# Nine product slots of block 1 placed in the opening stage, and a changed order of splits and loads in blocks 2 to 4

## The chip, the cores and the metric

The kernel runs on one core of a Trainium2 chip. The core has a matrix engine (TensorE, PE), a vector engine (VectorE, DVE), a scalar engine (ScalarE, ACT), GpSimd (POOL) and SyncE (SP), which in this kernel only issues transfers (DMAs). Each engine works through its own list of instructions in order and waits on semaphores for the others. The metric is the device time of one execution in microseconds; less is better.

## The reference

Chunked attention with a few memory keys, then two feed-forward networks. All arrays are float32.

```python
# attention: q, k, v are (4, 8, 768, 64); 8 memory keys and values per batch and head
for c in range(24):                       # chunks of 32 queries
    k_full = concat(mem_k, k[16 left .. 8 right of the chunk])       # 64 keys
    a = softmax(q_c @ k_full.T / 8)
    out[chunk] = a @ v_full
x = out as (3072, 512)
x = max(x @ w1, x @ w2, x @ w3) @ w_mid   # w1..w3 (512, 768), w_mid (768, 512)
h = x @ w_in                              # w_in (512, 2048)
g = h if h >= 1, 0 if h <= -1, else (h + 1)**2 / 4
out = g @ w_out                           # w_out (2048, 512)
```

## The kernel before

The 3072 tokens are six blocks of 512 (block 0 to 5). The attention runs in 24 units of 128 tokens, four units to a block. A unit u has steps, named by letter: s (scores, on TensorE), mx (the row maximum and its subtraction, on VectorE), ex (exp, ScalarE), n (sum and normalization), a with ca (transpose and copy, tile aT), o with co (product with the values, copy to xs), x with cx and dx (transposes tx, and the two parts xh and xl of the result, which the network reads). tk, ck, ek, kw and tq, c0q, c1q prepare keys and queries for units 0 to 11 by transposes on TensorE. From unit 12 (TRIO0) on, keys (three units at once, gk, tile kq) and queries (two units at once, gq) are loaded in pieces that VectorE transposes itself (flip_k, flip_q, steps fk and fq). Their loads are put into a list, `queue`, from which a few are issued in each slot; flip_k and flip_q issue what is left of the whole list before they begin.

Each product of the networks is made three times from numbers that are split in a high and a low part (mm3). A slot is 12 matmuls of 512 columns. For a block j of the first network a slot l1(j, f, m) makes the product with one of three weights (m = 0, 1, 2) for one of K1 = 6 groups of columns f; ScalarE copies the first to a tile t, VectorE takes the maximum of it and the second, and then the third, and the split makes hh (a cast on ScalarE) and hl (a subtraction on GpSimd) of t. A slot l2(j, f) adds the product of that with the weight b to four accumulators, y. The results of l1 lie in ps_mm, a pool of two PSUM buffers, in turn; a buffer is free again when the copy or the maximum has read it.

The weights come as float32 and are converted before use: convert_w (an abs, on ScalarE for some, then three operations on VectorE, tile c), then hi and lo parts by hi_w, rest_w and lo_w (VectorE, ScalarE and GpSimd). Block 0's and the later blocks' 24 weights (a0, a1, a2 and b, for f = 0 to 5) are converted in an opening stage whose order is the table PLAN. There l is an l1 slot of block 0 (l16 is f = 5, m = 1), lt its copy or maximum, lh its split, m an l2 slot, wa to wp the parts of a conversion, f a weight's load. TensorE's order is that of PLAN; the order on the other engines is set by a scheduler from the order of PLAN and its own estimate of times. Behind PLAN all engines keep the order in which the code is written.

Behind PLAN, a loop goes over the slots of blocks 1 to 5. In each slot of blocks 1 to 4 it makes one attention step (att_step) and one step of the second network's 32 weights, c and d (round_step): load, convert, round, and store to wd in DRAM. In block 5 and in the second network these are loaded again and split (w_step). SyncE issues everything in the order of the code.

```python
        for s, (f, *a) in enumerate(order):
            ...
            f(*a)
            if last_block:
                ...
            else:
                att_step()
                round_step()
```

Of the kernel before, what the change touches and what calls it, by code (L numbers as in the profile page):

```python
# [37 lines left out]

PLAN = """
# [25 lines left out]
SUM_ON_ACT = [2, 5, 6, 8]  # L65


@with_exitstack
def attention_then_two_mlps(ctx, tc, q, k, v, mem_k, mem_v, w1, w2, w3, w_mid, w_in, w_out, out):
# [229 lines left out]
    def load_ks(g):  # L299
        b, s0 = divmod(3 * g, UPB)  # L300
        t0 = s0 * P - LEFT
        c0 = 1 if t0 < 0 else 0
        for h in range(HP):
            for r, a in quadrants(k[b], h, t0 + c0 * CH, CH, NB3):
                queue.append(partial(nc.sync.dma_start, out=ks[r:r + CH, h, c0:c0 + NB3, :], in_=a))
        r0, c, t = (LEFT, 0, 0) if c0 else (0, NB3, S - LEFT)
        for e in range(2):
            for x in range(2):
# [3 lines left out]
                    in_=k[b].rearrange("(h e) t d -> e t h d", e=2)[e, t:t + LEFT, :, 32 * x:32 * x + 32]))  # L312

    def load_qs(g):
        b, s0 = divmod(2 * g, UPB)
        if 2 * g == TRIO0:
            t = stage.tile([P, TB, 2], U32, tag="st", name=f"qs{g}", bufs=3)
            t = t.rearrange("p f t -> p (f t)").bitcast(F32)
        else:
            t = kT2.rearrange("p i h t -> p (i h t)")[:, 0:2 * TB]  # L320
        qs[g] = t.rearrange("p (h c d) -> p h c d", h=HP, d=CH)
        for h in range(HP):
            for r, a in quadrants(q[b], h, s0 * P, CH, 2 * NC):
                queue.append(partial(nc.sync.dma_start, out=qs[g][r:r + CH, h], in_=a))
# [9 lines left out]
    def flip_q(u):  # L334
# [122 lines left out]
    def steps(u):  # L457
# [13 lines left out]
        if u == TRIO0 - 3 or u >= TRIO0 - 1 and u % 2:  # L471
            v += [("gq", (u + 3) // 2)]
# [30 lines left out]
    hs, cur, acc = {}, {}, {}  # L503

# [7 lines left out]
    def l1_pe(j, f, m):  # L512
        cur["ps", m] = ps = ps_mm.tile([P, TB], F32, tag="mm", name=f"l1_{j}_{f}_{m}")
# [99 lines left out]
    stash, slot = [], [1]  # L613

    def round_step():
        at_step = slot[0] % 6
        slot[0] += 1
        room = 4
        if at_step in (0, 2) and stash:
# [184 lines left out]
```

## Time and profile before

| | us |
|---|---|
| median of three runs (lowest, highest) | 1088.77 (1085.14, 1095.03) |
| the profiled execution | 1090.18 |
| span in its trace | 1088.1 |
| TensorE busy | 1034.8 (95%) |
| VectorE busy | 561.9 (52%) |
| ScalarE busy | 344.3 (32%) |
| GpSimd busy | 292.9 (27%) |

The mean granted clock of TensorE is 0.985 of full speed. On the chain of work that ended last, TensorE holds 82% and VectorE 11%. Busy shares are means over stages that differ much, so a stage has to be looked at by itself.

### The profile page before, as it was taken

How to read it: one execution, taken by the hardware profiler on the slowest of the kernel's cores; microseconds unless marked ns; L12 is line 12 of the kernel's file. 1: busy time of each engine (PE TensorE's matmuls, PEld its weight loads, DVE VectorE, ACT ScalarE, POOL GpSimd, SP SyncE). 2: the span in 40 equal slices, each digit the busy share in tenths (PEclk: the TensorE clock that was granted, in tenths of full speed). 3: DMA queues.
4: the chain of work that ended last, by engine and by line, in shares of the span. 5: the costliest groups of instructions: out<-in, count | busy, mean ns of one | idle time of the engine just before them, and what ended most of it. 6: DMA issues, size and time to landing. Idle time of an engine off the chain costs nothing.

```text
span 1088.1 us, 15214 instructions
## 1 busy us (share of the span) xinstructions
PE 1034.8 (95%) x5890; PEld 841.9 (77%) x5890; DVE 561.9 (52%) x883; ACT 344.3 (32%) x640; POOL 292.9 (27%) x233
## 2 busy tenths in 40 slices
PE   4887889999999999999999999999999999999998
PEld 3665668788778887888888888888888888888886
DVE  8899984678578777666454232223223223223222
ACT  5734434333223322224343222222222222222222
POOL 5465571010001110001223322322322332332221
PEclk8998999999999999999999999999999999999999
DMA  9745335446546456335441001001001001001001
GB/s 209 182 114 142 111 89 147 103 106 186 111 125 173 125 136 156 98 113 174 127 136 30 20 16 43 20 1 49 29 1 49 20 10 49 20 1 39 1 1 39
DMA packets 164504, 89.74 MB, mean 82 GB/s; under 512 B 126800, under 2 KB 144208, under 8 KB 164432
## 3 DMA queue, kind: packets, MB, share of 16 engines
q1 hardware_dynamic: 164432, 88.77, 30.2%
q8 instruction: 46, 0.75, 0.3%
q14 instruction: 26, 0.21, 0.1%
HBM read 67.76 MB, written 20.97 MB: 82 GB/s over the span
## 4 chain that ended last, share of the span: by engine, by line
PE 82%; DVE 11%; issue 2%; DMA 2%; SPq 2%; ACT 1%; POOL 0%; DVEq 0%; ACTq 0%; POOLq 0%
PE l L499 15%; PE l L500 15%; PE l L501 15%; PE o L590 8%; PE o L589 8%; PE o L588 8%; PE y L499 3%; PE y L500 2%; PE y L501 2%; PE s L358 2%; PE o L421 1%; DVE c_a L132 1%; DVE c_a L135 1%; SPq L328 1%; DMA st_d<-in_moe_w_out_dram 1%
## 5 line engine op out<-in xcount | busy, mean ns | idle before, releaser
L576 DVE SCALAR_TENSOR_TENSOR u<-u 128x512 f32<-128x512 f32 x96 | 66.5, 692 | 357.4 <-ACT u L575 357.4
L509 POOL TENSOR_TENSOR hl_b<-u,hh_b 128x512 fp32r<-128x512 f32 x96 | 123.8, 1290 | 373.6 <-ACT hh_b L508 209.8
L499 PE MATMUL l<-xh,hi_a 128*128 128x512 f32 x432 | 176.8, 409 | 7.8 <-DVE t L525 7.8
L501 PE MATMUL l<-xh,lo_a 128*128 128x512 f32 x432 | 170.4, 394 | 0.3 <-POOL lo_a L162 0.3
L500 PE MATMUL l<-xl,hi_a 128*128 128x512 f32 x432 | 170.3, 394 | 0.0
L499 PE MATMUL l<-yh,hi_c 128*128 128x512 f32 x384 | 150.5, 392 | 0.0
L500 PE MATMUL l<-yl,hi_c 128*128 128x512 f32 x384 | 150.4, 392 | 0.0
L501 PE MATMUL l<-yh,lo_c 128*128 128x512 f32 x384 | 150.3, 391 | 0.0
L590 PE MATMUL o<-hi_d,hl_b 128*128 128x512 f32 x384 | 150.0, 391 | 0.0
L588 PE MATMUL o<-hi_d,hh_b 128*128 128x512 f32 x384 | 149.9, 390 | 0.0
L589 PE MATMUL o<-lo_d,hh_b 128*128 128x512 f32 x384 | 149.9, 390 | 0.0
L509 POOL TENSOR_TENSOR hl_a<-t,hh_a 128x512 fp32r<-128x512 f32 x36 | 48.6, 1351 | 337.0 <-ACT hh_a L508 337.0
L575 ACT ACTIVATE u<-l 128x512 f32<-128x512 f32 x96 | 57.4, 598 | 240.3 <-PE l L501 197.7
L508 ACT CAST hh_b<-u 128x512 fp32r<-128x512 f32 x96 | 59.6, 621 | 143.7 <-DVE u L577 143.7
L499 PEld LDWEIGHTS l<-xh,hi_a 128*128 128x128 f32 x432 | 82.7, 191 | 26.3 <-DVE t L525 8.9
L501 PEld LDWEIGHTS l<-xh,lo_a 128*128 128x128 f32 x432 | 82.2, 190 | 18.6 <-POOL lo_a L162 0.7
L500 PEld LDWEIGHTS l<-xl,hi_a 128*128 128x128 f32 x432 | 82.7, 192 | 15.5
L501 PEld LDWEIGHTS l<-yh,lo_c 128*128 128x128 f32 x384 | 72.2, 188 | 15.9
L500 PEld LDWEIGHTS l<-yl,hi_c 128*128 128x128 f32 x384 | 72.2, 188 | 15.8
L588 PEld LDWEIGHTS o<-hi_d,hh_b 128*128 128x128 f32 x384 | 72.1, 188 | 15.7
L499 PEld LDWEIGHTS l<-yh,hi_c 128*128 128x128 f32 x384 | 72.1, 188 | 15.6
L590 PEld LDWEIGHTS o<-hi_d,hl_b 128*128 128x128 f32 x384 | 72.1, 188 | 15.5
(137 smaller groups left out, 1420.4 us busy)
## 6 DMA issues: line engine op xcount, KB each, us to landing
st_a<-in_moe_w_dram SPq DMA_DIRECT2D x18, 512.0 KB
vw<-in_v_dram SPq DMA_DIRECT2D x160, 56.0 KB
st_c<-in_moe_w_in_dram SPq DMA_DIRECT2D x16, 512.0 KB
st_d<-in_moe_w_out_dram SPq DMA_DIRECT2D x16, 512.0 KB
yd<-y SPq DMA_DIRECT2D x24, 256.0 KB
yr<-yd SPq DMA_DIRECT2D x24, 256.0 KB
out_dram<-ob SPq DMA_DIRECT2D x24, 256.0 KB
wd<-c_c SPq DMA_DIRECT2D x16, 256.0 KB
```

The source lines that it names most:

```text
L132: V.tensor_scalar(out=cf, in0=cf, scalar1=LEAST, scalar2=MOST, op0=ALU.max, op1=ALU.min)
L358: nc.tensor.matmul(sv[r:r + 64, c // 2, 2 * (h % 2) + h // 2, :], qTb[u % 2][:, h, c].rearrange("p e t -> p (e t)"), kw[:, h, c, 0:NK], st ...
L499: nc.tensor.matmul(ps, whi, xhi, start=first, stop=False)
L500: nc.tensor.matmul(ps, whi, xlo, start=False, stop=False)
L501: nc.tensor.matmul(ps, wlo, xhi, start=False, stop=last)
L508: nc.scalar.copy(out=hi, in_=h)
L509: nc.gpsimd.tensor_tensor(out=lo, in0=h, in1=hi.bitcast(F32), op=ALU.subtract)
L575: nc.scalar.activation(out=a, in_=ps, func=AF.Relu, bias=0.5, scale=0.5)
L576: nc.vector.scalar_tensor_tensor(out=a, in0=a, scalar=1.0, in1=a, op0=ALU.min, op1=ALU.mult)
L588: nc.tensor.matmul(acc[t], hi[:, c], whi, start=first, stop=False)
L589: nc.tensor.matmul(acc[t], hi[:, c], wlo, start=False, stop=False)
L590: nc.tensor.matmul(acc[t], lo[:, c], whi, start=False, stop=last)
```

## The change

The table PLAN gets nine slots of block 1, k0 to k8 (f = 0 to 2, m = 0 to 2), with their copies and maxima (kt) and one split (kh2). Unit 5 to 7 of the attention move forward in it, since block 1 needs them. Behind PLAN, block 1 has 15 slots left (nine of l1, m5 and five of l2), in an order written out by hand, and the attention's steps are spread over them, up to two in a slot. In blocks 2 to 4 the split of a tile t is issued a slot later, behind the attention's steps, and l2 stands behind the third l1 slot instead of ahead of it. Keys are put ahead of what waits in `queue`, queries have two buffers (kT2, and two tiles y) and are asked for in even units. The weights' steps follow two short tables, BY_SLOT and BY_PART; 28 of 32 weights are stored, and the last four are converted in the second network, by w_step.

```diff
-tk6 f7 cx3 wp5 wa7 dx2 a4 f8 wh7 wp6 dx3 wg7 l0 ca4 l1 wa8 lt0 ck6 wp7 f9 o4 lv5 wa9 lt1 s5 mx5 l2
+tk6 f7 cx3 wp5 wa7 dx2 a4 f8 wh7 wp6 dx3 wg7 l0 ca4 ck6 wp7 f9 lk8 ek6 wa8 lq7 l1 lt0 f10 wg8 wh8
...
+m2 wa15 cx7 dx7 wp14 k0 wg15 wh15 f17 l11 kt0 wp15 wa16 f18 l12 lt11 wg16 lh11 wh16 wa17 lt12 k1
...
+EARLY = 3
...
         c0 = 1 if t0 < 0 else 0
+        later = queue[:]
+        del queue[:]
         for h in range(HP):
...
+        queue.extend(later)
 
     def load_qs(g):
         b, s0 = divmod(2 * g, UPB)
-        if 2 * g == TRIO0:
-            t = stage.tile([P, TB, 2], U32, tag="st", name=f"qs{g}", bufs=3)
-            t = t.rearrange("p f t -> p (f t)").bitcast(F32)
+        if g % 2:
+            t = kT2.rearrange("p i h t -> p (i h t)")
+            t = [t[:, 0:TB], t[:, TB:2 * TB]]
         else:
-            t = kT2.rearrange("p i h t -> p (i h t)")[:, 0:2 * TB]
+            t = [mx.tile([P, TB], F32, tag="y", name=f"qs{g}_{i}", bufs=2) for i in range(2)]
...
-        if u == TRIO0 - 3 or u >= TRIO0 - 1 and u % 2:
-            v += [("gq", (u + 3) // 2)]
+        if u == TRIO0 - 3 or u >= TRIO0 - 2 and u % 2 == 0:
+            v += [("gq", u // 2 + 2)]
...
         if m == 0:
-            cur["t"] = mx.tile([P, TB], F32, tag="t", name=f"t_{j}_{f}", bufs=2)
-            nc.scalar.copy(out=cur["t"], in_=ps)
+            tag = "y" if j == 1 and f < EARLY else "t"
+            cur["t", j, f] = mx.tile([P, TB], F32, tag=tag, name=f"t_{j}_{f}", bufs=2)
+            nc.scalar.copy(out=cur["t", j, f], in_=ps)
...
     def slot_l1(j, f, m):
         l1_pe(j, f, m)
         l1_max(j, f, m)
-        l1_split(j, f, m)
+        if m == 2:
+            unsplit.append((j, f, m))
...
+    def feed(room):
+        while queue and room > 0:
+            queue.pop(0)()
+            room -= 1
...
+    def round_step(acts, most):
+        if "out" in acts and stash:
             n, t = stash.pop(0)
             nc.sync.dma_start(out=wd[n - len(round1)], in_=t)
-            room -= 1
-        if at_step in (0, 2) and fetched[0] < len(conv):
+        name = conv[converted[0]][0] if raw_tiles() else None
+        if "a" in acts and name and name not in half:
+            convert_w(*name)
+        if "b" in acts and name in half:
+            stash.append((converted[0], round_w(*name)))
+            converted[0] += 1
+        if "in" in acts and fetched[0] < stashed and raw_tiles() < most:
             fetch_w(*conv[fetched[0]][0])
             fetched[0] += 1
...
+    BY_PART = "out in b", "", "out in", "a", "b", "a"
+
+    BY_SLOT = "out a", "b in", ""
...
-        order = []
-        for j in range(1, NB):
+        order = [(slot_l1, 1, 3, 0), (slot_l2, 0, 5), (slot_l1, 1, 3, 1), (slot_l2, 1, 0),
+                 (slot_l1, 1, 3, 2), (slot_l2, 1, 1), (slot_l1, 1, 4, 0), (slot_l2, 1, 2),
+                 (slot_l1, 1, 4, 1), (slot_l1, 1, 4, 2), (slot_l2, 1, 3), (slot_l1, 1, 5, 0),
+                 (slot_l1, 1, 5, 1), (slot_l2, 1, 4), (slot_l1, 1, 5, 2)]
+        first2 = len(order)
+        for j in range(2, NB):
             for f in range(K1):
-                order += [(slot_l1, j, f, 0), (slot_l1, j, f, 1),
-                          (slot_l2, *((j, f - 1) if f else (j - 1, K1 - 1))), (slot_l1, j, f, 2)]
+                l2 = [(slot_l2, *((j, f - 1) if f else (j - 1, K1 - 1)))]
+                order += [(slot_l1, j, f, 0), (slot_l1, j, f, 1)]
+                order += [(slot_l1, j, f, 2)] + l2 if j < NB - 1 else l2 + [(slot_l1, j, f, 2)]
...
+            made = unsplit[:]
             f(*a)
+            if s in (1, 3):
+                l1_split(1, 1 + s // 2, 2)
+            if last_block:
+                made = unsplit[:]
+            else:
+
+                for _ in range(-(-(len(todo) - 6 * UB * (NB - 3) + 2) // (first2 - s)) if s < first2 else 1):
+                    att_step()
+
+            for x in made:
+                l1_split(*x)
+                unsplit.remove(x)
...
-                att_step()
-                round_step()
+                if s < first2:
+                    feed(4)
+                    round_step(BY_SLOT[s % 3], 1)
+                else:
+                    part = (slot[0] + 1) % 6
+                    slot[0] += 1
+                    feed((4, 5, 3, 5, 4, 0)[part])
+                    round_step(BY_PART[part], 3)
```

What the order becomes is shown at three places. First VectorE, at the end of the opening stage, before. The tiles c_b_4, c_a2_5 and c_b_5 are the last three weights; t_0_4 is block 0's tile for f = 4, and l1_0_4_2 the product that its last maximum reads.

```order
L525 TENSOR_TENSOR t_0_4_1427<-l1_0_4_2_1464,t_0_4_1427 128x512
L135 SCALAR_TENSOR_TENSOR c_b_4_1422<-st_b_4_1416,c_b_4_1422 128x512
L148 TENSOR_SCALAR st_b_4_1416<-c_b_4_1422 128x512
L154 SCALAR_TENSOR_TENSOR st_b_4_1416<-st_b_4_1416 128x512
L132 TENSOR_SCALAR c_a2_5_1477<-c_a2_5_1477 128x512
L133 TENSOR_SCALAR c_a2_5_1477<-c_a2_5_1477 128x512
L135 SCALAR_TENSOR_TENSOR c_a2_5_1477<-st_a2_5_1429,c_a2_5_1477 128x512
L148 TENSOR_SCALAR st_a2_5_1429<-c_a2_5_1477 128x512
L131 TENSOR_SCALAR c_b_5_1571<-st_b_5_1453 128x512
```

VectorE at the same place of the changed kernel:

```order
L137 SCALAR_TENSOR_TENSOR c_a2_5_1700<-st_a2_5_1606,c_a2_5_1700 128x512
L150 TENSOR_SCALAR st_a2_5_1606<-c_a2_5_1700 128x512
L133 TENSOR_SCALAR c_b_5_1725<-st_b_5_1663 128x512
L134 TENSOR_SCALAR c_b_5_1725<-c_b_5_1725 128x512
L135 TENSOR_SCALAR c_b_5_1725<-c_b_5_1725 128x512
L137 SCALAR_TENSOR_TENSOR c_b_5_1725<-st_b_5_1663,c_b_5_1725 128x512
L150 TENSOR_SCALAR st_b_5_1663<-c_b_5_1725 128x512
L533 TENSOR_TENSOR t_0_4_1457<-l1_0_4_2_1564,t_0_4_1457 128x512
L533 TENSOR_TENSOR t_1_1_1577<-l1_1_1_1_1589,t_1_1_1577 128x512
```

The last maximum of t_0_4 moved from ahead of these weights to behind the last of them, and maxima of block 1 follow it.

Second TensorE at unit 9's transposes ta9 in block 1, before; the other nine matmuls of l1_1_2_1 and then o9 follow.

```order
L500 MATMUL l1_1_2_0_1914<-xl1_864,hi_a0_2_723 128x512
L501 MATMUL l1_1_2_0_1914<-xh1_863,lo_a0_2_724 128x512
L409 MATMUL ta9_1929<-ident_81,p9_1847 128x128 x4
L499 MATMUL l1_1_2_1_1945<-xh1_863,hi_a1_2_866 128x512
L500 MATMUL l1_1_2_1_1945<-xl1_864,hi_a1_2_866 128x512
L501 MATMUL l1_1_2_1_1945<-xh1_863,lo_a1_2_867 128x512
```

TensorE at the same place of the changed kernel:

```order
L506 MATMUL l1_1_3_2_1984<-xl1_886,hi_a2_3_1349 128x512
L507 MATMUL l1_1_3_2_1984<-xh1_885,lo_a2_3_1350 128x512
L415 MATMUL ta9_1998<-ident_81,p9_1929 128x128 x4
L427 MATMUL o9_2005<-vw_90,aT9_2003 32x2x64 x16
L505 MATMUL y1_0_1932<-hh_a1_1_1847,hi_b_1_847 128x512
L506 MATMUL y1_0_1932<-hl_a1_1_1848,hi_b_1_847 128x512
L507 MATMUL y1_0_1932<-hh_a1_1_1847,lo_b_1_848 128x512
```

The product o9 reads the copy aT9 of ta9, and moved from a slot behind ta9 to right behind it.

Third SyncE in block 1, where keys and queries of units 12 and on are loaded, before: kq are keys, kT2 and qs queries, vw the values, st_d and st_c weights to be converted, wd the store of a rounded weight.

```order
L628 DMA kq_87<-in_k_dram 32x12x32 x10
L244 DMA vw_90<-in_v_dram 56x4x64 x6
L244 DMA vw_90<-in_v_dram 48x4x64 x2
L621 DMA wd_84<-c_d_0_2140 128x512
L112 DMA st_d_1_2262<-in_moe2_w_out_dram 128x1024
L628 DMA kq_87<-in_k_dram 32x12x32 x6
L328 DMA kq_87<-in_k_dram 16x4x32 x4
L621 DMA wd_84<-c_c_3_2219 128x512
L114 DMA st_c_4_2318<-in_moe2_w_in_dram 128x4x256
```

SyncE at the same place of the changed kernel:

```order
L246 DMA vw_90<-in_v_dram 56x4x64 x6
L246 DMA vw_90<-in_v_dram 48x4x64 x2
L630 DMA kq_87<-in_k_dram 32x12x32 x4
L333 DMA kq_87<-in_k_dram 32x12x32 x4
L333 DMA kq_87<-in_k_dram 16x4x32 x4
L333 DMA kT2_85<-in_q_dram 32x8x32 x16
L642 DMA wd_84<-c_c_1_2131 128x512
L114 DMA st_d_0_2321<-in_moe2_w_out_dram 128x1024
```

The load of a weight that stood between two parts of the keys now stands behind the rest of the keys and sixteen loads of queries. On VectorE the conversion of that weight, c_d_0, stands ahead of block 1's last maximum:

```order
L452 TENSOR_TENSOR xl2_1899<-tx11_2376,xh2_1898 128x4x128
L134 TENSOR_SCALAR c_d_0_2392<-c_d_0_2392 128x512
L135 TENSOR_SCALAR c_d_0_2392<-c_d_0_2392 128x512
L137 SCALAR_TENSOR_TENSOR c_d_0_2392<-st_d_0_2321,c_d_0_2392 128x512
L369 MEMSET s12_2409 64x4x16
L376 TENSOR_REDUCE m12_2427<-s12_2409 128x8
L381 TENSOR_TENSOR p12_2429<-s12_2409,m12_2427 128x512
L171 TENSOR_SCALAR st_d_0_2321<-c_d_0_2392 128x512
L172 SCALAR_TENSOR_TENSOR st_d_0_2321<-st_d_0_2321 128x512
L173 TENSOR_TENSOR c_d_0_2392<-c_d_0_2392,st_d_0_2321 128x512
L533 TENSOR_TENSOR t_1_5_2336<-l1_1_5_2_2437,t_1_5_2336 128x512
```

The buffer of l1_1_5_2, which this maximum reads, is the one that l1_2_0_1 takes next.

## Rows read from the trace of the kernel before

**Rows 1.** Busy us by stretch: PE, PEld, DVE, ACT, POOL, then granted clock, DMA.

```profile
50.00:100.00 50.00, 40.69 (x288) 32.30 (x287) 47.80 (x69) 20.30 (x54) 28.38 (x22) 0.97 0.48 130
100.00:150.00 50.00, 37.25 (x233) 28.92 (x234) 48.74 (x67) 18.78 (x41) 33.79 (x23) 0.91 0.45 125
...
600.00:700.00 100.00, 100.00 (x440) 82.26 (x439) 26.79 (x39) 26.12 (x44) 29.43 (x23) 1.00 0.08 26
```

**Rows 2.** Waits of TensorE: total us, times, longest.

```profile
PE tx L434 <- ACT xs L428: 10.2, 4, 3.6
```

**Rows 3.** Timeline of VectorE, end of the opening stage: start, us, what.

```profile
156.20 0.41 DVE L148 TENSOR_SCALAR st_b<-c_b 128x512 uint32<-128x512 uint32 x1
156.54 0.68 DVE L525 TENSOR_TENSOR t<-l,t 128x512 f32<-128x512 f32 x1
157.65 0.69 DVE L446 TENSOR_TENSOR xl<-tx,xh 128x512 fp32r<-128x512 f32 x1 [0.44 <-ACT xh L442]
158.26 0.68 DVE L370 TENSOR_REDUCE m<-s 128x8 f32<-128x512 f32 x1
158.97 0.17 DVE L373 TENSOR_SCALAR m<-m 128x8 f32<-128x8 f32 x1
```

**Rows 4.** Timeline of TensorE from block 1's first slot to block 2's.

```profile
160.87 0.39 PE L499 MATMUL l<-xh,hi_a 128*128 128x512 f32 x1
...
163.59 0.60 PE L252 MATMUL tk<-ident,kq 128*128 128x128 f32 x4
163.95 0.48 PE L499 MATMUL l<-xh,hi_a 128*128 128x512 f32 x1
...
169.98 0.60 PE L409 MATMUL ta<-ident,p 128*128 128x128 f32 x4
...
173.26 1.08 PE L421 MATMUL o<-vw,aT 128*32 128x128 f32 x32
...
242.87 0.50 PE L499 MATMUL l<-xh,hi_a 128*128 128x512 f32 x1
```

**Rows 5.** Timelines of SP, DVE, ACT and PE, block 2, 284 to 302 us.

```profile
284.50 12.04 SPq L328 DMA_DIRECT2D kq<-in_k_dram  x20
...
295.63 0.71 DVE L331 STREAM_TRANSPOSE kw<-kq 128x512 f32<-128x512 f32 x1 [6.58 <-DMA kq<-in_k_dram]
...
300.52 0.62 ACT L508 CAST hh_a<-t 128x512 fp32r<-128x512 f32 x1 [7.87 <-DVE t L525]
...
301.67 1.12 PE L434 MATMUL tx<-ident,xs 128*128 128x128 f32 x4 [3.56 <-ACT xs L428]
```

**Rows 6.** TensorE's second wait (timeline), and stretches after the first (columns as above).

```profile
424.73 1.11 PE L434 MATMUL tx<-ident,xs 128*128 128x128 f32 x4 [2.59 <-ACT xs L428]
...
302.00:304.00 2.00, 2.00 (x8) 1.71 (x7) 1.78 (x2) 1.28 (x3) 0.68 (x1) 0.50 0.17 36
304.00:306.00 2.00, 2.00 (x9) 1.63 (x8) 1.59 (x4) 0.00 (x0) 0.00 (x0) 0.84 0.84 256
```

**Rows 7.** One operation of the conversion: ns min/median/max, first and last start.

```profile
L132 DVE TENSOR_SCALAR c_a<-c_a x18: 409/848/1507, 11.0 to 146.9; 128x512 f32<-128x512 f32 x18
```

**Rows 8.** Timeline of VectorE: unit 8's copy aT.

```profile
170.62 0.69 DVE L413 COPY aT<-ta 128x512 f32<-128x512 f32 x1 [2.56 <-PE ta L409]
```

**Rows 9.** Timelines of SP and ACT: issues, and a weight's landing.

```profile
195.64 3.55 SPq L244 DMA_DIRECT2D vw<-in_v_dram  x8
...
270.98 4.78 SPq L628 DMA_DIRECT2D kT<-in_q_dram  x10
...
167.90 0.53 SPq L114 DMA_DIRECT2D st_c<-in_moe_w_in_dram  x1
...
172.86 0.67 ACT L129 ACTIVATE c_c<-st_c 128x512 f32<-128x512 f32 x1 [2.09 <-DMA st_c<-in_moe_w_in_dram]
```

**Rows 10.** Conversion of the weights d: ns min/median/max, first and last start.

```profile
L135 DVE SCALAR_TENSOR_TENSOR c_d<-st_d,c_d x16: 691/693/694, 214.3 to 499.2; 128x512 uint32<-128x512 uint32 x16
...
L169 DVE TENSOR_SCALAR st_d<-c_d x16: 417/418/421, 215.6 to 501.0; 128x512 uint32<-128x512 uint32 x16
L170 DVE SCALAR_TENSOR_TENSOR st_d<-st_d x16: 693/695/697, 216.0 to 501.5; 128x512 f32<-128x512 uint32 x16
L171 DVE TENSOR_TENSOR c_d<-c_d,st_d x16: 692/1648/1674, 216.7 to 502.2; 128x512 f32<-128x512 f32 x16
```

More of the change, by code (lines that the diff above doesn't have):

```diff
@@ L337, in flip_q @@
         c = u % 2 * NC
-        for e in range(2):
-            r = slice(e * 64, e * 64 + 64)
-            nc.vector.transpose(out=qTb[u % 2][r, :, :, e, :], in_=qs[u // 2][r, :, c:c + NC, :])
+        for i, t in enumerate(qs[u // 2]):
+            for e in range(2):
+                r = slice(e * 64, e * 64 + 64)
+                nc.vector.transpose(out=qTb[u % 2][r, 2 * i:2 * i + 2, :, e, :], in_=t[r, :, c:c + NC, :])
     def cp_q(u, e):
@@ L512, in l1_pe @@
     def l1_pe(j, f, m):
-        cur["ps", m] = ps = ps_mm.tile([P, TB], F32, tag="mm", name=f"l1_{j}_{f}_{m}")
+        cur["ps", j, m] = ps = ps_mm.tile([P, TB], F32, tag="mm", name=f"l1_{j}_{f}_{m}")
         whi, wlo = weights[f"a{m}", f]
@@ L544, in slot_l2 @@
             if f == K1 - 1:
-                if d < 2 or bp:
-                    y = (mx if d < 2 else bp["p"]).tile([P, TB], F32, tag="y", name=f"y_{j}_{d}", bufs=2)
+                if j == 0:
+                    y = (stage.tile([P, TB], F32, tag="c", name=f"y_{j}_{d}") if d < 2 else
+                         stage.tile([P, TB], F32, tag="st", name=f"y_{j}_{d}", bufs=3))
+                elif bp:
+                    y = (bp["p"], mx)[d // 2].tile([P, TB], F32, tag="y", name=f"y_{j}_{d}", bufs=2)
                 else:
@@ L610, in attention_then_two_mlps, with raw_tiles @@
     bp = {}
[L613 to L619, printed above, removed]
+    stash, slot = [], [0]
+    ready, asked = [len(round1)], [len(round1)]
+    def feed(room):
+        while queue and room > 0:
+            queue.pop(0)()
+            room -= 1
+    stashed = len(round1) + 28
+    def raw_tiles():
+        return fetched[0] - converted[0]
+    def round_step(acts, most):
+        if "out" in acts and stash:
@@ L624, in round_step, with w_tile, w_step @@
             fetch_w(*conv[fetched[0]][0])
             fetched[0] += 1
-            room -= 1
-        while queue and room > 0 and at_step != 5:
-            queue.pop(0)()
-            room -= 1
-        if at_step != 1 and at_step != 2 and converted[0] < fetched[0]:
-            n = converted[0]
+    BY_PART = "out in b", "", "out in", "a", "b", "a"
+    BY_SLOT = "out a", "b in", ""
+    def w_tile(n):
+        return conv[n][1] or bp["w"]
+    def w_step(s):
+        n = ready[0]
+        while asked[0] < min(stashed, n + 3) and asked[0] < converted[0] - len(stash):
+            load_w(asked[0])
+            asked[0] += 1
+        if n < asked[0]:
+            split_w(n, w_tile(n))
+            ready[0] += 1
+        elif n >= stashed and n < len(conv):
@@ L649, in attention_then_two_mlps @@
+                split_w(n, w_tile(n))
+                ready[0] = asked[0] = n + 1
+            if s % 3 == 0 and fetched[0] < len(conv) and fetched[0] == ready[0]:
+                fetch_w(*conv[fetched[0]][0])
+                fetched[0] += 1
+            elif s % 3 == 2 and name in staged:
+                convert_w(*name)
     later = ExitStack()
@@ L755, in attention_then_two_mlps @@
             else:
-                att_step()
-                round_step()
-        for f, *a in orderB:
+                if s < first2:
[6 more added lines that the diff above has]
+                    round_step(BY_PART[part], 3)
+        for x in unsplit:
+            l1_split(*x)
+        for s, (f, *a) in enumerate(orderB):
+            w_step(s)
             if f is slot_l3:
                 i, ff = a
-                while ("c", ff) not in weights or ("d", max(ff - 2, 0)) not in weights:
-                    w_step()
-                if i == 0:
-                    w_step()
+                assert ("c", ff) in weights and ("d", max(ff - 2, 0)) in weights
             f(*a)
```

47 lines of the change are left out of this document (20 added, 27 removed).

## The prediction

> **What bounds the kernel now.** I read the busy time by stretch first [rows 1]. From 600 to 700 us TensorE is busy for all of it at the full granted clock, and the other engines for under a third; after 600 us the view of TensorE's waits is empty. From 50 to 150 us TensorE idles for 22 of 100 us, and VectorE is busy for 96.5 of them: there VectorE converts block 0's weights and TensorE starves. So the kernel has two stages: a start of some 160 us that lasts as long as VectorE's list of work, and a rest that lasts as long as TensorE's. Nothing of the rest can shrink but its waits. The view of those waits [rows 2] has 10.2 us in which a transpose of an attention row (tx) waits for ScalarE's copy, and two of its four cases stand at 301.67 and 424.73 us, in blocks 2 and 3.
>
> The timelines show where the start ends. VectorE's last operation on a weight there ends at 156.6 us, and the max behind it at 157.2 [rows 3]. TensorE starts block 1 at 160.87 and block 2 at 242.87 us [rows 4]. Between these lie 24 slots of 12 matmuls and four attention units. A slot takes 163.59 - 160.87 = 2.72 us, about 2.8 with the start-up behind small work; a set of four transposes takes 163.95 - 163.59 = 0.36, o and s about 1.05 each (a busy row includes its drain).
>
> **Part 1: nine slots of block 1 in the start.** TensorE's total work stays as it is, so they gain only if TensorE is ahead when VectorE is done. They need all of unit 7 (xh1, xl1), whose copies move forward from 155 us past three weights or more. The order of the changed kernel shows the price on the other side. ps_mm has two buffers, and l1_0_5_0 takes the one of l1_0_4_2. That one is released by a max (t_0_4) which now stands on VectorE behind every conversion, where it stood ahead of the last three. So eight slots of the start (l1_0_5_0, _1, _2, m4 and four of block 1) can't run before VectorE's last conversion, however idle TensorE is. Counted from there, TensorE has 8 slots, and 15 more up to block 2: 23, where from 160.87 us it had 24. Nine slots moved in, but only one is gained: 2.8 us.
>
> When is that? VectorE does in the start all that it did, and ahead of the last conversion, in addition, unit 7's xl (0.69), unit 8's reduction and scaling (0.68 and 0.17) and two more operations as small as the scaling (some 0.4), and two maxes of block 1 for one of block 0 less (0.68 net). That is 2.6 us, less 0.2 since neighbours overlap by up to 0.1: 156.6 + 2.4 = 159.0, and then the max, 0.6 [rows 3]. TensorE goes on at about 159.6 instead of 160.87: 1.3 us gained. It will have waited there for some 5 us. After the 3.56 us wait at 301.67 the granted clock was 0.50, the 1.2 GHz level, for 2 us and 0.84 for 2 more, which loses 1.0 + 0.3 us [rows 5, 6]; I take the same 1.3. Part 1 thus gives 2.8 + 1.3 - 1.3 = **2.8 us**. Its bounds are wide, since VectorE's durations are not fixed: the same operation on the same size took 0.41 to 1.51 us, 0.85 in the middle [rows 7]. Eight weights lie behind unit 7's copies; at 0.44 us more or less for each, that is 3.5 us either way.
>
> **Part 2: attention in what is left of block 1.** 25 steps have to go into 15 slots, so ten slots take two. The pair that hurts is a and o: o now stands right behind the transposes ta, with no slot between, for units 8, 9 and 10. It needs the copy aT first. The copy starts 0.64 us after ta's start and takes 0.69 [rows 4, 8]; ta itself occupies TensorE for 0.36. So o waits 1.0 us, and a little more where ScalarE has a weight's abs ahead of the copy. Three times: **3.0 us lost**. Elsewhere a slot still stands between a step and the next. From s to ta there are two slots instead of three, 5.6 us and the small work, for a chain of reduction, subtraction, exp, sum and product, five operations of about 0.7 us with a handoff after each, some 5 us: covered, with little to spare. If that cover fails, a unit costs 1 to 2 us.
>
> The second cost is on SP. The queue of loads is flushed when unit 12's keys are needed, which is now three slots after they were asked for. Counted from the end of o10: eight loads of v, 3.6; twelve of keys at 0.60, 7.2; sixteen of queries at 0.48, 7.7; two more, 0.8; then weight d_0 is asked for and lands 5.0 us after its issue: 24.3 us [rows 5, 9]. ScalarE's abs of d_0 (0.67), three VectorE operations (0.41 twice and 0.69), m12 and p12 (0.68 each), three for the rounding (0.42, 0.69, 0.69) and the max t_1_5 (0.68) follow in order: 30.3 us, handoffs and overlaps set against each other [rows 3, 7, 9, 10]. The last of the rounding took 1.65 as often as not, where it met GpSimd; I take the low end, since GpSimd's split waits for the same max here. TensorE gets to l1_1_5_2's successor but one, l1_2_0_1, which needs that max, after eight slots (22.4) and 4.2 us of small work: 26.6 us. It waits **3.7 us**, and loses 1.3 to the clock: 5.0. The bounds are 0 (SP finds no wait ahead of the keys and issues them sooner) and 8 (the rounding collides, and the load takes as long again).
>
> **Part 3: blocks 2 to 4.** The wait at 301.67 us is one chain [rows 5]: SP issues twenty loads of keys in 12.04 us; VectorE waits 6.58 us for them in the transposes to kw; so its max t is late; ScalarE's cast hh waits 7.87 us for t, and the copy xs stands behind the cast in ScalarE's order; the tx transposes wait 3.56 us. Each link is cut now: keys are queued ahead of queries, queries have two buffers and are asked for earlier, and the cast comes a slot later, behind the copy. The same holds for the 2.59 us at 424.73 [rows 6]. With 1.3 us of clock each this gives 3.56 + 2.59 + 2.6 = 8.8 us; **8.8 us gained**. What is late next? The split feeds a product three slots on, and GpSimd has nothing else there, so I cost the delay at nothing; without that cover it would cost a slot, 2.8 us, at most once a block. The loads of weights are now up to three ahead, which hides them there.
>
> **Part 4: the end.** Four weights are converted in the last stage instead of being stored before. VectorE is busy 27% there [rows 1]; their nine operations or so fit in its gaps. Nothing. Bounds: 0 and 2 us, if a load is late in ScalarE's order.
>
> **The sum.** -2.8 + 3.0 + 5.0 - 8.8 = -3.6 us, on the profiled execution's 1090.18: 1086.6. That execution lay 1.4 us above the median of the three runs, so 1088.77 - 3.6 = **1085.2** is my forecast, by its own bounds 1079 to 1091. Most of what the change wins in blocks 2 and 3, it pays back in block 1.
>
> **Rivals.** First, VectorE's list shrinks. GpSimd works 62 of 100 us beside it in the start [rows 1], and where the two overlap less, an operation takes 0.41 instead of up to 1.51 us [rows 7]. Eight weights with one such operation each: up to 8.8 us sooner, and TensorE, which would be waiting anyway, takes all of it: 1076. For it: the spread is real. Against it: the operations of both engines are the same and as dense. The Trainium skill (SBUF — State Buffer, Who interferes with whom) says that VectorE and GpSimd share a pair of ports under an exclusive lock that is held for a whole instruction, and that the order of issue decides who waits. By that rule a new order may move this stretch either way, with the same work; the trace agrees, with 0.41 against 1.51 us. Chance 0.13.
>
> Second, block 1's price is not paid: d_0 lands in time since SP runs ahead, and only the gaps before o stay: 1085.2 - 5.0 = 1080; without the gaps too, 1077. For it: SP's part of my sum is made from issues that each stood in a busier queue, and a load that is issued 4 us sooner costs nothing. Against: the 19 us are issue time alone, with no wait in them. Chance 0.17.
>
> Third, slower: units 5 to 7 are pulled forward in VectorE's list, and there each has operations that wait in order for TensorE, ScalarE or GpSimd; VectorE has no idle time now, so every such wait delays the last conversion and all behind it. A late link of a chain cost 3.56 us at 301.67. Three units at that price, 10.7 us: 1096. It decides when the last conversion ends later than 159.0 + 3.6 = 162.6 us; from there the kernel is slower than before. For it: 2 to 3 us of such waits I can already see in the order (the sum and the abs behind unit 7's chain), inside my bounds. Against: the rows ahead of each mostly cover it. Chance 0.14.
>
> Fourth, the change doesn't do what it says: the new order moves the waits of blocks 2 and 3 rather than ends them. 1085.2 + 8.8 = 1094. The loads of keys start four slots sooner, so I give it 0.06.
>
> **How the numbers follow.** The forecast has 0.50. One per cent is 10.9 us, about what a measurement here can tell from no change (the three runs span 9.9 us). Below 1077.9: of the first rival 0.10, half of the second 0.09, the forecast's low end 0.09: 0.28. Above 1099.7: a third of the third rival 0.05, the ends of the others 0.05: 0.10. Between: 0.62. The range for 8 in 10 reaches from the first two rivals to the third: 1074 to 1096.
>
> **What would show it.** The last conversion on VectorE near 159 us, and then a max that TensorE waits for (part 1; at 150 the first rival, at 163 the third). Three waits of o for aT of about 1 us between 180 and 220 us, and one of l1 for t_1_5 of some 4 us near 246 (part 2). No wait of tx for xs behind 250 us, and the clock at 1.00 throughout (part 3). The prediction is wrong if TensorE takes up block 2 more than 5 us away from 242.87 - 2.8 + 3.0 = 243.1 us, or if a new wait stands in blocks 2 to 4.

## The result, and the profile after

The changed kernel takes **1098.24 us** (median of 8 runs, 1096.59 to 1103.36), beside 1090.35 for the kernel before (8 runs, 1085.14 to 1095.03). The ratio is 1.0083, with an interval of 1.0053 to 1.0112: slower by 0.8%, where I had forecast 1085.2 and a range up to 1096. The profiled execution took 1103.36 us with a span of 1101.4. It lies 5.1 us above its kernel's median, the one of before near its own, so the sums below, made from the two traces, speak of 13.3 us and not of 7.9. No trace shows an execution of the changed kernel at its median.

The span can be cut where TensorE takes up block 2. Before, that was at 242.87 us [rows 4] and 845.2 us were left. After, it is this row of TensorE's timeline (start, duration, operation), and 1101.4 - 256.18 = 845.2 us are left too:

```profile
256.18 0.39 PE L505 MATMUL l<-xh,hi_a 128*128 128x512 f32 x1
```

So in this trace all 13.3 us arise before block 2, and of the 8.8 us that blocks 2 to 4 were to gain nothing is left. Two causes have to be found. (An estimate for the other executions: the second trace of this kernel, e6 below, has block 2 at 254.4 us. If the start is as long in all of them, the median of 1098.24 us, less the 2 us by which the time is longer than the span, leaves some 840 to 842 us behind it, so a part of the gain may be there in most.)

**The start.** VectorE's timeline at its end answers to [rows 3]:

```profile
170.35 1.67 DVE L137 SCALAR_TENSOR_TENSOR c_b<-st_b,c_b 128x512 uint32<-128x512 uint32 x1
172.05 0.43 DVE L150 TENSOR_SCALAR st_b<-c_b 128x512 uint32<-128x512 uint32 x1
172.39 0.68 DVE L533 TENSOR_TENSOR t<-l,t 128x512 f32<-128x512 f32 x1
```

The last conversion ends at 172.5 us, not at 159.0. Is that more work or more waiting? The busy time by stretch says it, up to this point in the changed kernel (its columns are length, then busy us and count of PE, PEld, DVE, ACT and POOL, then clock, DMA share and GB/s):

```profile
0.00:172.50 172.50, 125.87 (x1003) 100.36 (x1004) 147.72 (x234) 77.95 (x182) 90.72 (x79) 0.89 0.52 133
100.00:150.00 50.00, 41.99 (x290) 33.08 (x289) 40.49 (x59) 16.51 (x42) 23.92 (x19) 0.91 0.36 103
```

VectorE is busy 147.7 us and idle 24.8. In the kernel before, up to the end of its last conversion:

```profile
0.00:156.60 156.60, 114.28 (x948) 90.82 (x949) 146.38 (x228) 74.08 (x164) 92.44 (x78) 0.92 0.58 147
```

There it was busy 146.4 us and idle 10.2. So the work grew by 1.3 us and the idle time by 14.6 (by 12.5 in e6). The second row of the changed kernel shows it from the other side: 40.49 of 50 us where [rows 1] has a VectorE that hardly stops. Its timeline names what it waited for (in brackets: idle time ahead of the row, and who ended it):

```profile
105.99 0.69 DVE L533 TENSOR_TENSOR t<-l,t 128x512 f32<-128x512 f32 x1 [2.18 <-PE l L507]
106.97 0.68 DVE L353 COPY qTb<-tq 64x512 f32<-64x512 f32 x1 [0.29 <-ACT qTb L353]
110.22 0.69 DVE L376 TENSOR_REDUCE m<-s 128x8 f32<-128x512 f32 x1 [2.56 <-PE s L364]
110.95 0.69 DVE L381 TENSOR_TENSOR p<-s,m 128x512 f32<-128x512 f32 x1
112.39 0.69 DVE L402 TENSOR_REDUCE r<-p 128x8 f32<-128x512 f32 x1 [0.76 <-ACT p L394]
...
122.67 1.25 DVE L133 TENSOR_SCALAR c_a<-st_a 128x512 uint32<-128x512 uint32 x1 [1.18 <-POOL lo_b L164]
...
141.43 0.78 DVE L403 TENSOR_SCALAR r<-r 128x8 f32<-128x8 f32 x1 [1.77 <-ACT p L390]
...
151.07 0.43 DVE L133 TENSOR_SCALAR c_a<-st_a 128x512 uint32<-128x512 uint32 x1 [1.20 <-POOL lo_a L164]
```

At 106.97 to 112.39 and at 141.43 us these are steps of units 7 and 8 (5.4 us of waiting), and at 105.99 a max of block 0 (2.18). They now stand between the weights, each behind a partner that was not ready. At 122.67 and 151.07 us a weight itself waits until GpSimd has read the one before in its tile (2.4). From 104 to 114 us VectorE converts no weight at all, although one could have come: b_2's load was issued at 89.98 us, a tile c came free at 97.9, and e4 below starts this weight at 101.00 us without a wait.

**Blocks 2 to 4.** TensorE's waits behind the start, from its timeline:

```profile
168.66 0.80 PE L505 MATMUL l<-xh,hi_a 128*128 128x512 f32 x1 [4.79 <-ACT t L531]
203.45 1.41 PE L427 MATMUL o<-vw,aT 128*32 128x128 f32 x32 [0.83 <-ACT y L561]
217.11 1.39 PE L427 MATMUL o<-vw,aT 128*32 128x128 f32 x32 [0.71 <-ACT aT L419]
230.31 1.39 PE L427 MATMUL o<-vw,aT 128*32 128x128 f32 x32 [0.73 <-DMA kq<-in_k_dram]
260.34 0.50 PE L505 MATMUL l<-xh,hi_a 128*128 128x512 f32 x1 [1.28 <-ACT t L531]
264.31 0.63 PE L415 MATMUL ta<-ident,p 128*128 128x128 f32 x4 [0.95 <-DVE p L406]
386.87 1.09 PE L415 MATMUL ta<-ident,p 128*128 128x128 f32 x4 [3.47 <-DVE p L406]
620.30 0.50 PE L505 MATMUL l<-yh,hi_c 128*128 128x512 f32 x1 [0.81 <-DVE u L589]
```

The waits of tx for xs at 301 and 424 us [rows 5, 6] are gone. A new one has come at 386.87, and it costs twice, as the windows behind it show in the clock's column:

```profile
387.00:389.00 2.00, 2.00 (x7) 1.75 (x8) 1.93 (x4) 0.59 (x1) 0.00 (x0) 0.50 0.25 39
389.00:391.00 2.00, 2.00 (x6) 1.57 (x5) 1.93 (x5) 0.00 (x0) 0.00 (x0) 0.50 0.80 199
391.00:393.00 2.00, 2.00 (x17) 1.35 (x20) 1.34 (x3) 0.00 (x0) 0.00 (x0) 0.69 1.00 273
```

3.47 us idle and 1.0 + 1.0 + 0.6 us of slow clock make 6.1. Its chain is read backwards over four engines:

```profile
367.83 7.76 SPq L333 DMA_DIRECT2D qs<-in_q_dram  x15
376.13 0.43 SPq L114 DMA_DIRECT2D st_d<-in_moe_w_out_dram  x1
381.70 0.66 ACT L131 ACTIVATE c_d<-st_d 128x512 f32<-128x512 f32 x1 [1.82 <-DMA st_d<-in_moe_w_out_dram]
382.40 0.43 DVE L134 TENSOR_SCALAR c_d<-c_d 128x512 f32<-128x512 f32 x1 [3.18 <-DMA vw<-in_v_dram]
386.03 0.69 DVE L406 TENSOR_TENSOR p<-p,r 128x512 f32<-128x512 f32 x1
```

SP issues fifteen loads of queries at a stretch; a weight's load is asked for behind them and its abs is late; VectorE, which has this weight's three operations ahead of the unit's sum and product, waits 3.18 us (the row names a transfer that landed last, but the operation needs c_d, which ScalarE had just written). These queries were not needed there: flip_k and flip_q issue all that is queued, and the queue held the queries of units 20 and 21, while the keys of unit 18 were wanted.

### The profile page after: what moved, and what is told of

It is laid out like the page before. It is cut to its first block, busy times and chain, and to the rows that moved or that the text cites. A ratio compares the mean times of both kernels' runs of the same rounds, so it can differ in the third digit from the quotient of the medians.

```text
span 1101.4 us, 15218 instructions
## 1 busy us (share of the span) xinstructions
PE 1042.2 (95%) x5890; PEld 847.6 (77%) x5890; DVE 574.8 (52%) x907; ACT 343.8 (31%) x640; POOL 291.7 (26%) x233
## 4 chain that ended last, share of the span: by engine, by line
PE 78%; DVE 12%; ACT 3%; DMA 3%; SPq 2%; issue 2%; POOL 0%; DVEq 0%; ACTq 0%; POOLq 0%
PE l L505 15%; PE l L507 15%; PE l L506 15%; PE o L600 7%; PE o L602 7%; PE o L601 7%; PE y L505 2%; PE y L506 2%; PE y L507 2%; PE s L364 2%; PE o L427 1%; DVE c_a L137 1%; SPq L630 1%; DVE c_a L134 1%; DMA st_c<-in_moe_w_in_dram 1%
```

## The experiments

Theory A: the start's loss is VectorE's waiting in its own order, mostly for pulled-forward attention, and the gain of blocks 2 to 4 is lost to flushes of the queue. Theory B: the loss is elsewhere, in the edits of blocks 2 to 4, in the squeezed attention, or in TensorE's own chain. The table has what decided; "busy" and "idle" are VectorE's up to the end of the last conversion, "block 2" is its start, "rest" is from there to the end of the span. All columns but the ratio are us of one trace.

| kernel | ratio to before (interval) | last conversion | busy, idle | block 2 | rest |
|---|---|---|---|---|---|
| before | 1 | 156.6 | 146.4, 10.2 | 242.9 | 845.2 |
| changed | 1.0083 (1.0053 to 1.0112) | 172.5 | 147.7, 24.8 | 256.2 | 845.2 |
| e1, old start | 0.9933 (0.9911 to 0.9955) | 156.9 | 146.4, 10.5 | 243.4 | 840.3 |
| e2, needed loads | 1.0034 (1.0016 to 1.0052) | 172.2 | 147.3, 24.9 | 255.9 | 838.2 |
| e3, squeeze alone | 0.9990 (0.9972 to 1.0008) | 159.3 | 146.2, 13.1 | 248.6 | 840.9 |
| e4, one weight moved | 1.0021 (1.0003 to 1.0039) | 167.2 | 145.4, 21.8 | 250.2 | 840.9 |
| e5, e1 with e2 | 0.9919 (0.9901 to 0.9936) | 156.7 | 146.3, 10.4 | 242.8 | 836.4 |
| e6, changed again | 1.0088 (1.0070 to 1.0107) | 170.7 | 148.0, 22.7 | 254.4 | 846.5 |
| e7, e2 with e4 | 0.9983 (0.9967 to 1.0000) | 165.8 | 144.6, 21.2 | 250.0 | 838.7 |
| e8, e3 with e2 | 0.9961 (0.9948 to 0.9975) | 157.2 | 146.3, 10.9 | 246.5 | 838.3 |
| e9, e5 with six abs moved | 0.9904 (0.9883 to 0.9925) | 155.0 | 142.0, 13.0 | 242.6 | 837.1 |

**e1: the old start under the new blocks 2 to 4.** (In the edits, words in parentheses stand for a long table, and "..." for lines left out.)

```diff
 PLAN = (the table of the kernel before)
-EARLY = 3
+EARLY = 0
...
-        order = [(slot_l1, 1, 3, 0), (slot_l2, 0, 5), ...]
-        first2 = len(order)
+        order = []
+        for f in range(K1):
+            order += [(slot_l1, 1, f, 0), (slot_l1, 1, f, 1),
+                      (slot_l2, *((1, f - 1) if f else (0, K1 - 1))), (slot_l1, 1, f, 2)]
+        first2 = 0
...
-            if s in (1, 3):
-                l1_split(1, 1 + s // 2, 2)
```

> The start and block 1 are the order of the kernel before (its PLAN, no product slot of block 1 in the start, one attention step per slot); only the edits of blocks 2 to 4 and of the end stay. Theory A (the loss is the start's: VectorE waits 14.2 us more there, in order, for TensorE, ScalarE and GpSimd): the last conversion is back near 157 us, block 2 starts near 243 us, and what is left is the gain of blocks 2 to 4, between the 2.7 us that the changed kernel shows there (8.9 us of idle time and slow clock from 250 to 500 us before, 8.4 after, less 2.2 of these that belong to block 1) and the 8.8 us of my prediction: 1081.5 to 1087.7 us, ratio 0.992 to 0.998 to before. Theory B (the edits of blocks 2 to 4 cost time, and the start's delay would have been made up): 1094 or more, ratio above 1.003.

1083.28 us: faster than both kernels, within what theory A gave, and theory B falls for the edits of blocks 2 to 4. One wait was left there, and SP's row ahead of it has the same form as at 367.83 us above:

```profile
369.97 0.61 PE L505 MATMUL l<-xh,hi_a 128*128 128x512 f32 x1 [1.92 <-ACT t L531]
```
```profile
352.15 7.36 SPq L333 DMA_DIRECT2D qs<-in_q_dram  x15
```

**e2: issue only what is needed.** Each queued load carries the name of its group:

```diff
+    def issue_all(x):
+        while any(y == x for y, _ in queue):
+            queue.pop(0)[1]()
...
     def flip_k(u):
-        while queue:
-            queue.pop(0)()
+        issue_all("k")
...
     def flip_q(u):
-        while queue:
-            queue.pop(0)()
+        issue_all(u // 2)
```

> The changed kernel, but a flush of SP's queue of loads issues only what is needed next: the queries of units 12, 13 and of 20, 21 are no longer issued in one piece (16 and 15 of them) when the keys or queries of a unit before are needed. Theory A (the wait of 3.47 us of ta for p at 386.87 us is SP's: 7.76 us of query issues stand ahead of the load of a weight d, whose abs on ScalarE is late, so that three VectorE operations on it stand late ahead of the sum and the product of p): that wait and the slow clock behind it go, 3.5 + 2.7 = 6.2 us, and the 2.2 us at 260 to 265 us may go too: 1098.2 - 6.2 to - 8.4 = 1090 to 1092 us, ratio 0.9995 to 1.0015 to before. Rival (VectorE has too much ahead of p in that stretch whatever SP does): a wait of ta for p stays there, shorter by less than half, and the ratio stays at 1.005 or above.

1094.99 us. The order of the instructions differs from the changed kernel's in two places on SP alone; the weight's load is issued at 370.00 instead of 376.13 us, and the waits shrink:

```profile
259.53 0.50 PE L507 MATMUL l<-xh,hi_a 128*128 128x512 f32 x1 [0.73 <-ACT t L533]
382.07 0.63 PE L417 MATMUL ta<-ident,p 128*128 128x128 f32 x4 [0.61 <-DVE p L408]
```

The rest falls from 845.2 to 838.2 us. SP's order is the only thing that differs and the ratio falls from 1.0083 to 1.0034, with intervals apart, so the flush costs time. By the ratios that is some 5 us, by the medians 3.3, where I had expected 6.2 to 8.4. How much of it the wait at 386.87 us was, is not as clear (see e6).

**e3: the squeeze without the pulling forward.**

```diff
 PLAN = (the table of the kernel before) + """
+k0 kt0 k1 kt1 k2 kt2 k3 kh2 kt3 k4 kt4 k5 kt5 k6 kt6 k7 kt7 k8 kt8
 """
```

> The start in the order of the kernel before up to its end, then the nine slots of block 1 in a row, then block 1 with two attention steps in ten of its fifteen slots, and blocks 2 to 4 as in the changed kernel. So attention is squeezed as in the change, but no unit is pulled forward in VectorE's list. Theory A: the last conversion is near 157 us as before; the squeeze costs what the changed kernel shows in 175 to 300 us, 4.5 us of idle time against 2.2: 2 to 4 us with a d_0 that may come late; blocks 2 to 4 gain some 2.7: 1088 to 1092 us, ratio 0.998 to 1.002. Theory B (squeezing attention into block 1 is the loss): 1097 or more, ratio above 1.006.

1091.18 us, as theory A gave, and theory B falls for the squeeze as the main loss. This run takes back two things at once, the units pulled forward and block 1's slots between the weights, and none of the runs tells them apart. TensorE's waits in block 1 are those of the changed kernel, with d_0's somewhat longer:

```profile
195.82 1.41 PE L427 MATMUL o<-vw,aT 128*32 128x128 f32 x32 [0.83 <-ACT y L561]
...
253.81 0.50 PE L505 MATMUL l<-xh,hi_a 128*128 128x512 f32 x1 [2.34 <-ACT t L531]
257.79 0.63 PE L415 MATMUL ta<-ident,p 128*128 128x128 f32 x4 [0.94 <-DVE p L406]
```

**e4: one weight in the gap.** In PLAN one name moves:

```diff
-... wh11 n6 wh12 wp11 ck9 s7 ek9 wg12 a6 kw8 ... n7 l9 lv7 co6 wa14 wa13 lt9 ...
+... wh11 n6 wh12 wp11 ck9 wa13 s7 ek9 wg12 a6 kw8 ... n7 l9 lv7 co6 wa14 lt9 ...
```

> The changed kernel, with the conversion of one weight, b_2 (six VectorE operations, some 3.3 us without contention), moved ahead of the maxes and the softmax of unit 7, where VectorE waited 2.18, 0.29, 2.56 and 0.76 us between 104 and 112 us. Nothing else moves but this weight's cast and GpSimd's pair behind it. Theory A (VectorE's waits in its own order set the end of the start): about 3.3 us of these waits are filled, the last conversion ends 3 to 5 us sooner than 172.4, and the time falls by the same: 1093 to 1095 us, ratio 1.003 to 1.005 to before. Rival (TensorE's own chain of unit 7, o7 to xs7 to tx7, sets the end of the start, and VectorE would only wait elsewhere): the waits come back behind unit 7, the last conversion stays within 1.5 us, and the ratio stays at 1.007 to 1.009.

1092.64 us: six operations, moved ahead of eight others on VectorE, are worth about 0.6% of the whole, more than the 3 to 5 us that I had expected. VectorE's rows in the place that was shown above:

```profile
104.07 0.69 DVE L156 SCALAR_TENSOR_TENSOR st_b<-st_b 128x512 f32<-128x512 uint32 x1
105.41 0.69 DVE L533 TENSOR_TENSOR t<-l,t 128x512 f32<-128x512 f32 x1 [0.64 <-PE l L507]
...
109.63 0.69 DVE L376 TENSOR_REDUCE m<-s 128x8 f32<-128x512 f32 x1 [2.55 <-PE s L364]
...
115.41 0.57 DVE L134 TENSOR_SCALAR c_a<-c_a 128x512 f32<-128x512 f32 x1 [1.75 <-ACT c_a L131]
```

The max waits 0.64 instead of 2.18 us, unit 7's scores are waited for as before, and a new wait of 1.75 us comes behind: a weight moved ahead leaves VectorE with nothing ready a little later. Still the last conversion is 5.3 us sooner, and TensorE goes on at 163.38 instead of 168.66. Not all of that is waiting: VectorE's idle time fell by 3.0 us and its busy time by 2.3. The six operations themselves took 5.4 us at 114 to 121 us in the changed kernel, and 3.6 us at 101 to 105 here, where GpSimd stood idle from 101.64 to 104.31. The rival, TensorE's chain of unit 7, falls. Part of the 0.6% is not this: the wait at 386.87 is 0.48 us here, at 379.09.

**e5: e1 and e2 together.**

> The kernel of e1 (start and block 1 as before, blocks 2 to 4 and the end as changed) with the flush of e2 (only the loads that are needed next are issued). In e1 one wait is left in blocks 2 to 4, 1.92 us at 369.97 us with 1.72 us of slow clock behind it; there SP issued 15 loads of queries in 7.36 us ahead of a weight's load, ScalarE waited 5.14 us for that weight and VectorE 2.80 for ScalarE. Theory A (the flush is its cause): it goes, 1083.3 - 1.9 to - 3.6 = 1079.7 to 1081.4 us, ratio 0.990 to 0.992 to before, faster than both kernels. Rival (the queue is as full without the flush and the weight's load as late): the ratio stays at 0.993.

1082.44 us, the fastest so far by its ratio, though its interval overlaps that of e1. In its trace TensorE has no wait between the end of the start and the second network; these are the last two rows of its timeline with a wait:

```profile
156.42 0.66 PE L442 MATMUL tx<-ident,xs 128*128 128x128 f32 x4 [2.73 <-DVE xs L436]
598.11 0.50 PE L507 MATMUL l<-yh,hi_c 128*128 128x512 f32 x1 [0.79 <-DVE u L591]
```

The rest is 836.4 us, 8.8 less than before: as much as the term of my part 3, once the flush is out of its way. It is one trace, and 0.9 us of the trace before went to a slow clock at its very end, which part 3 has nothing to do with.

e1 and e5 settle a rival for the start, too. TensorE's granted clock over the whole start was 0.92 in the kernel before and 0.89 in the changed one, so the slower clock could be what delayed VectorE. But e1 had 0.89 and e5 0.93 with one order of the start, and their last conversions end at 156.9 and 156.7 us.

**e6: the changed kernel once more.** No edit.

> The changed kernel itself, once more. Of its eight times two are at 1103.3 us and six between 1096.6 and 1099.5, and the profiled one is one of the two. The wait at 386.87 us with the slow clock behind it is 6.2 us, and e4, which does not touch that place, shows only 0.48 us there. Theory A (this wait is at the edge and comes in some executions only, and most of the gain forecast for blocks 2 to 4 is there in the others): most times between 1096 and 1100, and a profile with under 1 us of wait of ta for p near 382 us. Rival (it is in every execution, and e4's later stages moved past it): the profile shows about 3.5 us there again. Either way the ratio is 1.005 to 1.010.

1100.68 us (1098.16 to 1103.51), and my theory of a wait that comes in some executions only is not borne out:

```profile
260.61 0.71 PE L505 MATMUL l<-xh,hi_a 128*128 128x512 f32 x1 [3.32 <-ACT t L531]
387.43 1.09 PE L415 MATMUL ta<-ident,p 128*128 128x128 f32 x4 [3.31 <-DVE p L406]
```

Both traces of this kernel have it, but both are of executions above their median. e4 and e3, with the same orders and the same flush there, show 0.48 and 0.61 us, no more than e2 without the flush. Two rows of e4 beside 376.13 and 381.70 us above show what differs:

```profile
369.83 0.43 SPq L114 DMA_DIRECT2D st_d<-in_moe_w_out_dram  x1
373.92 0.64 ACT L131 ACTIVATE c_d<-st_d 128x512 f32<-128x512 f32 x1
```

ScalarE read the weight 4.1 us after its issue (4.2 in e3), and did not wait for it; in the changed kernel and here it was 5.6 and 5.7 us, and ScalarE waited. So the flush leaves the load no room, and in these four traces its time to land decides whether TensorE waits. Why it took longer in two of them, and whether the faster executions have the wait, stays open.

**e7: e2 and e4 together.**

> The changed kernel with both edits, e2's (only the loads needed next) and e4's (one weight's conversion ahead of unit 7's softmax). Theory A (two separate causes): e4's wait of 2.12 us at 255 us and its 1.41 us of slow clock go, 1092.6 - 3.5 = 1089 us, ratio 0.998 to 0.9995. Rival (one edit only pays for what the other does): 1091.5 to 1093, ratio 1.001 to 1.002.

1090.11 us. Against e2, which differs by the moved weight alone, the ratio falls by 0.51% (5.6 us) and block 2 starts 5.95 us sooner; against e4, which differs by the flush alone, by 0.38%. The two causes nearly add up: 0.49 and 0.62% each by itself, 1.00% together.

**e8: e3 with e2.**

> The kernel of e3 (start as before, nine slots in a row, then attention squeezed into fifteen slots) with e2's flush. Theory A: of the squeeze's cost the part that is SP's goes, 2.34 us of l1 for t at 253.81 us and 0.94 of ta for p behind it; the three waits of o for the copy ahead of it, 0.83, 0.72 and 0.73 us, stay, since there is no slot between: 1091.2 - 2 to - 3.3 = 1088 to 1089 us, ratio 0.996 to 0.998, so that against e5 the squeeze still costs more than these 2.3 us. Rival (the weight d_0 is late for want of time, not for the flush): the wait for t stays over 2 us, and the ratio at 0.999.

1087.55 us. TensorE's waits in this stretch:

```profile
193.72 1.44 PE L429 MATMUL o<-vw,aT 128*32 128x128 f32 x32 [0.83 <-ACT y L563]
207.38 1.47 PE L429 MATMUL o<-vw,aT 128*32 128x128 f32 x32 [0.71 <-ACT aT L421]
220.64 1.39 PE L429 MATMUL o<-vw,aT 128*32 128x128 f32 x32 [0.73 <-DMA kq<-in_k_dram]
250.09 0.50 PE L507 MATMUL l<-xh,hi_a 128*128 128x512 f32 x1 [0.73 <-ACT t L533]
```

Of the wait at 253.81 us 0.73 is left, so the late d_0 was SP's flush. Nine slots moved ahead and the squeeze cost 3.7 us at block 2's start against e5 (246.5 to 242.8), of which the three waits of o are 2.3, and 0.4% of the time.

**e9: work off VectorE's list.** To e5's ABS_ON_ACT six names are added:

```diff
-ABS_ON_ACT = "a0.2 a0.3 a0.5 a1.1 a2.1 a2.2 a2.3 a2.5 b.0 b.4".split()
+ABS_ON_ACT = "a0.2 a0.3 a0.4 a0.5 a1.1 a1.3 a1.4 a1.5 a2.1 a2.2 a2.3 a2.4 a2.5 b.0 b.3 b.4".split()
```

> The kernel of e5 with the abs of six more weights of the start (a0_4, a1_3, a1_4, a1_5, a2_4, b_3) taken from VectorE and given to ScalarE; nothing else is edited, the scheduler shifts some neighbours by a place or two. It asks the other half of theory A: that the start is as long as VectorE's work and waits together. An abs took 0.41 to 1.54 us on VectorE in e5, so six are some 3 to 5 us of its work. If the work goes and no wait comes for it: the last conversion ends 3 to 5 us sooner than 156.7, and the time is 1077.5 to 1079.5 us, ratio 0.987 to 0.989 to before. Rival (VectorE now waits in order for ScalarE's abs, as it waited for ScalarE and GpSimd in the changed kernel, so that work off its list turns into idle time on it): VectorE's idle time before the last conversion grows by 3 us or more from 10.6, and the ratio stays at 0.991 to 0.993, or is above.

1080.78 us, not told apart from e5. Of the 4.3 us of work that went 2.6 came back as idle time, most of it in one row of VectorE:

```profile
111.12 0.43 DVE L134 TENSOR_SCALAR c_a<-c_a 128x512 f32<-128x512 f32 x1 [2.51 <-ACT c_a L131]
```

The last conversion ends 1.7 us sooner, but block 2 starts at 242.55 instead of 242.82 us. So neither expectation holds: VectorE's list is shorter and the time is the same. What holds the start up then, I have not tried; unit 7's xl stands at 157.47 us on VectorE, beside 157.74 in e5, and the slots of block 1 need it.

## Why the prediction was wrong, step by step

**Part 1, the step that failed.** "When is that?" was answered with VectorE's operations alone, 2.6 us of them, and 159.0 came out. The work was sized well enough (1.3 us measured). The waits were left to the bounds, as "2 to 3 us" that "the rows ahead of each mostly cover". They grew by 14.6 us. I had written the mechanism down as the third rival, with its deciding point at 162.6 us, and the last conversion ended at 172.5; its time, 1096, came near in part by chance, with 10.7 us for the 14.6 and part 3's gain counted in full. I gave it 0.14. My reason against it, cover by the rows ahead, could have been tested on the order: behind xl of unit 5 it has no weight until unit 7's sum, so nothing could cover those waits. e4 shows that such a row was worth having. And part 1's bounds took an operation's duration to be what varies; 3.5 us either way was too narrow for waits.

**The slot gained.** I had TensorE stop at l1_0_5_0, for the max of t_0_4. It stopped one slot earlier: from 168.66 us there are 24 slots to block 2, as before. The wait was for ScalarE's copy of t_1_1, which stands behind a weight's cast that waited 4.37 us for VectorE. So the gain of 2.8 us was not there either. From the forecast for block 2, 243.1, to 256.2 us: TensorE goes on 9.1 us later than 159.6, has a slot more (2.8), and loses 2.6 us to the clock instead of 1.3; the waits of o take back 0.7. That is 12.5 of the 13.1 us.

**Part 2** was right in its mechanisms but for one link. The three waits of o were 2.3 us instead of 3.0. The weight d_0 came late by the very chain that I had summed, and e2 and e8 show it, but it cost 2.2 us in the changed kernel, not 5.0, and TensorE waited for the copy of t_2_0 behind unit 12's exp rather than for the max t_1_5:

```profile
259.71 0.57 ACT L531 COPY t<-l 128x512 f32<-128x512 f32 x1
260.85 0.68 DVE L533 TENSOR_TENSOR t<-l,t 128x512 f32<-128x512 f32 x1
```

l1_2_0_1 began at 260.34 us, right behind the copy and ahead of the max, and it did so in e3 and e4 too. So it did not wait for the buffer that this max reads: the sentence on that buffer under the change, and the prediction's use of it, do not hold.

**Part 3** was right in what it removes and blind to what comes next, the fourth rival's mechanism (0.06). I had costed the flush of sixteen queries in block 1, and did not ask where else keys and queries are asked for in the same unit. They are at units 10 and 16, and the second is the wait at 386.87 us: 6.1 us in this trace; whether the faster executions have it is open (e6). With the flush mended the gain is 8.8 us (e5).

**Part 4:** one wait of 0.81 us at 620.30, inside its bounds.

## What to carry to other kernels

An engine that is the bound and hardly idle has two ways to get slower, and a sum of its operations sees one of them: before moving a chain with partners on other engines into its list, look up for each moved row which independent row can stand ahead of it, and when its partner is ready. A flush of a shared queue should issue what is needed and no more, since everything behind it, weights above all, pays for the rest. Cutting a program at a landmark, such as the first product of a block, tells at once which stage a difference belongs to.

## What was not expected of the hardware

The clock costs more than I took from the kernel before. After the wait of 4.79 us TensorE worked at a granted clock of 0.50 for 168 to 172 us and 0.55 for the next two, a loss of 2.6 us, and behind the 3.47 us at 386.87 the loss was the same; I had 1.3 from [rows 6], which leave out the third of a us ahead of 302.00; with it the trace before has 1.5. In e6, behind 3.32 and 3.31 us, it was about 1.7 and 1.5, and behind 2.34 us in e3 nothing, so the price of a wait is not fixed by its length. Behind the waits of 0.6 to 0.8 us in e2 the windows show 1.00. VectorE's busy time changes with the order at the same work: 147.7 and 148.0 us up to the last conversion in the two traces of the changed kernel, 145.4 in e4, which differs on VectorE by the place of one weight. The Trainium skill (SBUF — State Buffer, Who interferes with whom) has VectorE and GpSimd share ports under an exclusive lock. The traces agree with an effect of order, and at 2.3 to 2.6 us it is far below the 8.8 that my first rival gave it.
